# The first stage of the kernels' transform with cosines and sines in one matmul, and a store in four parts

## The chip, the cores and the metric

The kernel runs on one core of a Trainium2 chip. The metric is the device time of one execution in microseconds; lower is better. A profile is one execution taken by the hardware profiler; its span runs from the first to the last recorded work.

## What is computed

A state-space convolution and a gated unit work on the same normalised input and are added to it. L is 2048, D 448, N 256, F 1792.

```python
xn = layernorm(x)                                   # [1, 2048, 448]
P = exp((A * dt[:, None])[:, :, None] * pos)        # A, C complex [448, 256]
K = 2.0 * einsum("dn,dnl->dl", C, P).real           # one kernel of 2048 taps per channel
y = irfft(rfft(xn.T, 4096) * rfft(K, 4096))[:, :2048].T + xn * D_skip
h = sigmoid(xn @ w_gate) * (xn @ w_up)
out = x + y + h @ w_down
```

## The kernel before

Two generators are woven into one program: conv() makes the kernels K and convolves, glu() does the gated unit. A planner takes the next piece from the one whose share of its planned work is smaller, and a scheduler then sets the order of each engine's instructions from priorities and estimated times. An engine runs its instructions strictly in that order. The matmuls of glu() (gu on L685, po on L792) thus fill TensorE between those of conv().

kgen() makes the kernels in 56 chunks of 8 channels. A chunk takes phases from DRAM by matmul (tr, L517), gets sines and cosines of them on ScalarE (S, L526 to L529), magnitudes from GpSimd and ScalarE (me, mf, pm), products on VectorE (Et on L579 and L580, Ft on L581), and sums over N by matmul into a bank ko of PSUM (L593). S is made one chunk ahead of its use.

Four chunks, 32 channels, fill a bank; there are 14 banks. ScalarE copies ko to ks (L606), and first_stage(bank) (L532 to L551) does the first step of the kernels' Fourier transform. The 2048 taps are 32 values of a times 64 of b. ks has 64 r + 32 j + a on partitions, and 8 groups s of 64 values of b, so a channel of the bank is (s, r, j). A matmul holds ks[rows, s], 64 x 64, in the array and streams wk[rows, cc], 64 rows x 64 columns: for the two channels j the 32 frequencies k of a table, which is cosines for cc = 0 and sines for cc = 1. The results go to two banks of PSUM, kp for r = 0 and kq for r = 1, at partitions 64 cc + b. Each matmul of float32 is two instructions in the profile. Two copies on ScalarE (L550) put them into sk as [128, k, (s r j)], 32 x 32, and one store on ScalarE's queue (L551) writes sk to sk_d[:, bank], 4 KB per partition.

spectra() begins after the last bank. Its step for k = 4, ..., or the single step 32, is fed by loads() through SP's queue: sx (x1_d, the transform of the input), tb (a table), and skl (sk_d; 7 banks, four frequencies, 32 channels: runs of 512 B, L849). Step 32 reads one frequency of the rows 64 to 127 in two loads of 64 x 7 x 32 (L841). Step 32 is the second of 17, and its loads are the first that read the last bank. loads() runs three steps ahead. there() multiplies tb with skl and sx (sp, L874), ScalarE and VectorE form the product of the spectra, and back() and last() transform back.

The names that the change touches: sk, sk_d, pss (kp and kq) and first_stage in kgen(); skl, loads() and there() in spectra().

Of the kernel before, what the change touches and what calls it, by code (L numbers as in the profile page):

```python
# [11 lines left out]
F32 = mybir.dt.float32  # L12
# [8 lines left out]
D = 448  # L21
# [28 lines left out]
NLD = 3  # L50
# [80 lines left out]
def s4d_glu_kernel(ctx, tc, io):  # L131
    nc = tc.nc
# [6 lines left out]
    dram = ctx.enter_context(tc.tile_pool(name="dram", bufs=1, space=DRAM))  # L139
    acc_d = dram.tile([128, 8, D], F32, name="acc_d")  # L140
    ph_d = dram.tile([D, 6, N], F32, name="ph_d")
    x1_d = dram.tile([64, NB, D], F32, name="x1_d")
    sk_d = dram.tile([128, D // 32, 32, 32], F32, name="sk_d")
    wt_d = dram.tile([2, NFT, 128, 8 * 128], F32, name="wt_d")

    v_d = dram.tile([2, 128, 32, H], F32, name="v_d")
# [5 lines left out]
    wk = const.tile([128, 2, 128], F32, name="wk")[:, :, :64]  # L152
# [25 lines left out]
    psg = ctx.enter_context(tc.tile_pool(name="psg", bufs=1, space=PSUM))  # L178
# [257 lines left out]
    def kgen(pk):  # L436
        fts, mls, sins = [], [], []

        late = [
            ("sk", [128, 32, 32], F32), ("ks", [128, 8, 64], F32),  # L440
            ("me1", [128, 4 * DC, 64], F32), ("mf1", [128, 4 * DC, 32], F32),
            ("S1", [128, 5, 2 * DC, 32], F32), ("Et1", [128, 2, 2 * DC, 64], F32),
            ("Et0", [128, 2, 2 * DC, 64], F32), ("Ft", [128, 2, 2 * DC, 32], F32),
# [4 lines left out]
        tl = {n: pk.tile(sh, dt_, name=n) for n, sh, dt_ in late}  # L448
# [82 lines left out]

        def first_stage(bank):  # L532

            ks, sk = tl["ks"], tl["sk"].rearrange("p k (s r j) -> p r k s j", r=2, j=2)

            pss = [
                psc[-1].tile([128, 8, 2, 32], F32, name="kp", bufs=1),
                psg.tile([128, 8, 2, 32], F32, name="kq", tag="gu", bufs=4),
            ]
            for s_ in range(8):  # L540
                for cc in range(2):
                    for r in range(2):
                        rows = slice(64 * r, 64 * r + 64)
                        nc.tensor.matmul(  # L544
                            pss[r][64 * cc : 64 * cc + 64, s_].rearrange("p j k -> p (j k)"),
                            ks[rows, s_], wk[rows, cc], start=True, stop=True,
                            skip_group_check=True,
                        )
            for r in range(2):
                nc.scalar.copy(sk[:, r], pss[r].rearrange("p s j k -> p k s j"))  # L550
            nc.scalar.dma_start(sk_d[:, bank], tl["sk"])  # L551

        with hp(HP):
            phase_load(0)
# [8 lines left out]
        for g in range(NCK // NCH):  # L563
            for c in range(NCH):
# [23 lines left out]
                for q in range(2):  # L588
                    sl = 2 * (cn % 4) + q
                    for k in range(4):  # L590
                        h, cc = k // 2, k % 2
                        for j in range(4):
# [4 lines left out]
                                start=(k == 0),  # L597
                                stop=(k == 3),
                                skip_group_check=True,
                            )  # L600
                if cn % 4 == 3:
                    ks = tl["ks"]
# [5 lines left out]
                if cn % 4 == 2 and cn > 3 or cn + 1 == NCK:  # L608

                    with hp(HP) if cn + 1 == NCK else tc.issue_after(glu_mm[0].ins):  # L610
                        first_stage((cn - 3) // 4 if cn + 1 < NCK else cn // 4)
# [202 lines left out]
    def spectra(pf):  # L814
# [15 lines left out]
        def work(n, sh, bufs):  # L830
            return spare[n].pop() if spare[n] else pf.tile(sh, F32, name=n, bufs=bufs)


        def loads(h, k):
            sx = pf.tile([128, 4, H], F32, name="sx", bufs=NLD)
            sk = pf.tile([128, 7, 4, 32], F32, name="skl", bufs=NLD)
            if k == 32:

                nc.sync.dma_start(sx[:64, 0:2].rearrange("b h d -> b (h d)"), x1_d[32])
                for i in range(2):  # L840
                    nc.sync.dma_start(sk[:64, :, i], sk_d[64:, 7 * i : 7 * i + 7, 0])  # L841
                return t32, sk, sx
            ds, gs = slice(H * h, H * h + H), slice(7 * h, 7 * h + 7)
            nc.sync.dma_start(sx[0:64], x1_d[k : k + 4, :, ds].rearrange("k b d -> b k d"))
            nc.sync.dma_start(sx[64:128], x1_d[32 + k : 36 + k, :, ds].rearrange("k b d -> b k d"))
            tb = pf.tile([128, 4, 128], F32, name="tb", bufs=NLD)
            nc.sync.dma_start(tb, io["c_tab"][k // 4])

            nc.sync.dma_start(sk, sk_d[:, gs, k : k + 4])  # L849
            return tb, sk, sx  # L850

        def bank(name):
            return psc[-1].tile([128, 2, H], F32, name=name, tag="sp", bufs=4)

        def after():
            return tc.issue_after(sp_mm[0].ins)

        def there(k, tb, sk, sx):

            kk, np_ = (64, 64) if k == 32 else (128, 128)  # L860
            ys_ = []
            for j in range(2):

                ks = [(0, j, 0)] if k == 32 else [(2 * j + i, 2 * j + i, i) for i in range(2)]
                pss = []
                for src in (sk, sx):
                    ps = bank("sp")
                    with after():
                        for c in range(2):
                            for t, n, i in ks:  # L870
                                to, rhs = ps[64 * i : 64 * i + 64, c], sx[:kk, n]
                                if src is sk:
                                    to, rhs = to.rearrange("p (g d) -> p g d", d=32), sk[:kk, :, n]
                                mm = nc.tensor.matmul(  # L874
                                    to, tb[:kk, t, 64 * c : 64 * c + 64], rhs, start=True, stop=True,
                                    skip_group_check=True,
                                )
                    sp_mm[:] = [mm]
                    pss.append(ps)
                    if src is sk:  # L880
                        kc = work("kc", [128, 2, H], 3)
                        nc.scalar.copy(kc[:np_], ps[:np_])
                yy, pd = work("yy", [128, 2, H], 4), work("pd", [128, 2, H], 2)
                xt = pss[1]
                v.tensor_tensor(yy[:np_], kc[:np_], xt[:np_], ALU.mult)
                v.tensor_tensor(pd[:np_], kc[:np_], xt[:np_, ::-1], ALU.mult)
                v.tensor_tensor(yy[:np_, 0], yy[:np_, 0], yy[:np_, 1], ALU.subtract)
                v.tensor_tensor(yy[:np_, 1], pd[:np_, 0], pd[:np_, 1], ALU.add)
                ys_.append(yy)
            return ys_  # L890
# [63 lines left out]

        steps[0:2] = [steps[1], (None, 32), steps[0]]
        ld = [loads(*s) for s in steps[:NLD]]
        nc.gpsimd.dma_start(wf, io["c_wf"])
        prev, wait, due = None, [], []
        sp_mm[:] = glu_mm
        for n, (h, k) in enumerate(steps):  # L960

            sp_mm[:] = glu_mm
            if prev is not None:
                back(*prev)
            cur = there(k, *ld[n])
            if n + NLD < len(steps):
                ld.append(loads(*steps[n + NLD]))
            if 4 <= n < 8:
                o = slice(2 * n - 8, 2 * n - 6)
                nc.sync.dma_start(ac[:, o], acc_d[:, o])  # L970
            if due and n >= due[0]:
                for m in (0, 2, 4, 6)[2 * (n - due[0]) : 2 * (n - due[0]) + 2]:
                    last(0, m)
                if n == due[0] + 1:
                    due = []
            if prev is not None and prev[1] < 32:
                wait.append(prev[:2])

            while len(wait) > 1 and not (due and wait[0][0] == 1):
                t = wait.pop(0)  # L980
                turned(*t)
                if t == (0, 28):
                    due = [n + 1]
            prev = (h, k, cur)
            glu_on[:] = [1]
            yield WS
# [5 lines left out]
    def conv():  # L992
        with tc.tile_pool(name="psk", bufs=1, space=PSUM) as ps_, tc.tile_pool(
# [78 lines left out]
            with tc.tile_pool(name="pk", bufs=1, side="right", reuse_waits="tile") as pk:  # L1072
                yield from kgen(pk)
# [9 lines left out]
    xq, psc, raws, acl, marks, slots, pqs = list(x_first), [], [], [], [None, None], {}, []  # L1083
# [6 lines left out]
    while any(g is not None for g in gens):  # L1090
# [3 lines left out]
        i = min(live, key=lambda i: done[i] / total[i])  # L1094
# [33 lines left out]
```

## Time and profile before

| what | us |
|---|---|
| median of 3 runs | 756.99 (754.02 to 760.32) |
| the profiled execution | 754.25 |
| its span | 752.5 |

| engine | busy us | share |
|---|---|---|
| TensorE, matmuls | 702.7 | 93% |
| TensorE, loads of weights | 553.0 | 73% |
| VectorE | 560.3 | 74% |
| ScalarE | 423.2 | 56% |
| GpSimd | 346.2 | 46% |

The mean granted clock of TensorE was 0.983 of full speed. In the profile PE is the matmuls of TensorE, PEld its loads of weights, DVE VectorE, ACT ScalarE, POOL GpSimd, SP the SyncE; a q behind an engine's name means its instruction queue, as in ACTq for a DMA that ScalarE issues. Issuing a DMA is not counted as busy. The lines of a group have the form: line, engine, operation, output <- inputs, count, durations. The durations of matmuls are modelled from start to end and overlap, so the distance between starts says more than the duration of one. q10 in the table of DMA queues carries the DMAs that ScalarE issues, q1 those of SP, q0 those of GpSimd.

### The profile page before, as it was taken

The numbers are of one execution on the slowest core, as the hardware profiler recorded it, in microseconds if no ns is written. First come the engines' busy times: TensorE is split into PE (matmuls) and PEld (weight loads), VectorE is DVE, ScalarE is ACT, GpSimd is POOL, SyncE is SP. The second block draws the span as 40 slices with busy tenths as digits, with TensorE's granted clock in tenths as the row PEclk, the third lists the DMA queues.
The fourth block names the chain that finished last, engine by engine and source line by source line (L and its number), as shares of the span: only waits on it lengthen the run. The fifth ranks groups of instructions, "written<-read, shape, count | busy, mean of one in ns | idle before, by whom it ended". The sixth has DMA issues, their size and how long they took to land.

```text
span 752.5 us, 19365 instructions
## 1 busy us (share of the span) xinstructions
PE 702.7 (93%) x7892; PEld 553.0 (73%) x7892; DVE 560.3 (74%) x776; ACT 423.2 (56%) x650; POOL 346.2 (46%) x423
## 2 busy tenths in 40 slices
PE   2897999988998999999999999999899999998994
PEld 2675888766876788655888888888777787776783
DVE  5799996897878898888578968977864555564553
ACT  3546374767677778977487677676643222322310
POOL 2100055995484867863557566566545001341001
PEclk9999999997999999999999999999999999999998
DMA  9945457234223433465852222131158999999746
GB/s 205 232 136 156 121 158 220 68 127 157 70 71 127 156 122 115 123 181 155 245 163 98 74 103 91 64 101 63 49 152 246 255 250 239 240 246 242 184 125 170
DMA packets 90761, 114.75 MB, mean 152 GB/s; under 512 B 11889, under 2 KB 78641, under 8 KB 90417
## 3 DMA queue, kind: packets, MB, share of 16 engines
q1 hardware_dynamic: 81360, 92.78, 45.2%
q10 hardware_dynamic: 6736, 14.57, 6.4%
q0 software_dynamic: 2576, 6.17, 3.1%
q8 instruction: 62, 1.02, 0.6%
q14 instruction: 27, 0.21, 0.1%
HBM read 69.64 MB, written 43.84 MB: 151 GB/s over the span
## 4 chain that ended last, share of the span: by engine, by line
PE 62%; DMA 13%; DVE 10%; ACT 5%; issue 3%; POOL 3%; SPq 2%; POOLq 0%; ACTq 0%; DVEq 0%
PE gu L685 25%; PE po L792 13%; PE tr L517 7%; PE ko L593 6%; PE sp L874 4%; PE pv L901 3%; DMA sx<-x_d 2%; DMA vp<-v_d 2%; DVE hl L703 1%; DMA skl<-sk_d 1%; DMA xe<-in_A_u_dram 1%; DMA tb<-in_c_tab_dram 1%; PE kp L544 1%; DMA v_d<-vt 1%; DMA aim<-in_A_A_imag_dram 1%
## 5 line engine op out<-in xcount | busy, mean ns | idle before, releaser
L494 POOL TENSOR_TENSOR me<-me,pm 128x32 f32<-128x32 f32 (+1 forms) x168 | 138.3, 823 | 111.0 <-DVE Et L580 91.5
L494 POOL TENSOR_TENSOR mf<-mf,pm 128x64 f32<-128x64 f32 (+1 forms) x112 | 107.5, 960 | 4.2
L685 PE MATMUL gu<-xh,wh 128*128 128x512 f32 x336 | 99.8, 404 | 2.2 <-DVE xl L213 2.2
L685 PE MATMUL gu<-xh,wl 128*128 128x512 f32 x336 | 96.6, 393 | 0.0
L685 PE MATMUL gu<-xl,wh 128*128 128x512 f32 x336 | 96.1, 391 | 0.0
L579 DVE TENSOR_TENSOR Et<-me,S 128x1024 f32<-128x1024 f32 x56 | 77.1, 1378 | 17.9 <-ACT S L529 17.9
L580 DVE TENSOR_TENSOR Et<-me,S 128x1024 f32<-128x1024 f32 x56 | 77.1, 1376 | 16.1 <-ACT me L507 12.3
L792 PE MATMUL po<-dh,hh 128*128 128x448 f32 x224 | 85.0, 379 | 2.6 <-DVE hf L696 1.3
L526 ACT ACTIVATE S<-tr 128x1024 f32<-128x1024 f32 x56 | 57.6, 1028 | 52.4 <-PE tr L517 47.0
L581 DVE TENSOR_TENSOR Ft<-mf,S 128x1024 f32<-128x1024 f32 x56 | 81.0, 1446 | 6.4 <-ACT S L529 4.1
L792 PE MATMUL po<-dl,hh 128*128 128x448 f32 x224 | 82.9, 370 | 0.0
L792 PE MATMUL po<-dh,hl 128*128 128x448 f32 x224 | 81.9, 367 | 0.0
L685 PEld LDWEIGHTS gu<-xh,wh 128*128 128x128 f32 x336 | 61.5, 190 | 20.6 <-issue 4.4
L593 PEld LDWEIGHTS ko<-Et,Ft 128*32 128x32 f32 x3584 | 55.1, 112 | 27.5 <-issue 16.9
L701 ACT CAST hh<-hf 128x512 fp32r<-128x512 f32 x56 | 35.0, 625 | 70.3 <-DVE hf L696 59.0
L685 PEld LDWEIGHTS gu<-xh,wl 128*128 128x128 f32 x336 | 63.3, 189 | 14.4 <-issue 0.7
L593 PE MATMUL ko<-Et,Ft 128*32 128x64 f32 x3584 | 65.6, 224 | 8.7 <-DVE Ft L581 4.8
L685 PEld LDWEIGHTS gu<-xl,wh 128*128 128x128 f32 x336 | 62.8, 188 | 14.1 <-issue 0.7
L696 DVE SCALAR_TENSOR_TENSOR hf<-th,gu 128x512 f32<-128x512 f32 x56 | 38.1, 681 | 40.6 <-PE gu L685 37.1
L797 DVE SCALAR_TENSOR_TENSOR acc<-po,acc 128x448 f32<-128x448 f32 x80 | 48.5, 618 | 25.9 <-PE po L792 25.7
L517 PE MATMUL tr<-sel,ph 128*128 128x512 f32 x224 | 66.6, 418 | 1.1 <-ACT S L528 0.6
L529 ACT ACTIVATE S<-S,hpi 128x1024 f32<-128x1024 f32 x56 | 65.5, 1169 | 0.0
(186 smaller groups left out, 1299.4 us busy)
## 6 DMA issues: line engine op xcount, KB each, us to landing
sk_d<-sk ACTq DMA_DIRECT2D x14, 512.0 KB
sx<-x_d SPq DMA_DIRECT2D x32, 224.0 KB
skl<-sk_d SPq DMA_DIRECT2D x16, 448.0 KB
vp<-v_d SPq DMA_DIRECT2D x16, 448.0 KB
v_d<-vt SPq DMA_DIRECT2D x62, 112.0 KB
wt_d<-wh SPq DMA_DIRECT2D x9, 512.0 KB
wt_d<-wl SPq DMA_DIRECT2D x9, 512.0 KB
wh<-wt_d SPq DMA_DIRECT2D x9, 512.0 KB
```

Of the source, the lines that this page charges most:

```text
L494: ins = nc.gpsimd.tensor_tensor(m[:, :, w + a : 2 * w : n], m[:, :, a:w:n], par(base + i).unsqueeze(2).to_broadcast([128, 4 * DC, w // n]) ...
L517: nc.tensor.matmul(ps[:, h], ph[:, cn % 2, 128 * h : 128 * h + 128], sel[:, i], start=(i == 0), stop=(i == 1),)
L526: nc.scalar.activation(rows(cs), pv, AF.Abs)
L529: sins[:] = [nc.scalar.activation(cs, cs, AF.Sin, scale=-TWO_PI, bias=hpi)]
L579: v.tensor_tensor(Et[:, :, :, 32:64], two(me[:, :, 32:64]), S[:, 1::-1], ALU.mult)
L580: v.tensor_tensor(Et[:, :, :, 0:32], two(me[:, :, 0:32]), S[:, 1:3, :, ::-1], ALU.mult)
L581: fts[:] = [v.tensor_tensor(Ft, two(mf), S[:, 3:5], ALU.mult)]
L593: mm = nc.tensor.matmul(ko[32 * j : 32 * j + 32, sl], Ft[:, cc, DC * h + 4 * q + j], Et[:, cc, DC * h + 4 * q + j], start=(k == 0), stop=( ...
L685: glu_mm[:] = [nc.tensor.matmul(ps, a_, b_, start=(n == 0), stop=(n == len(mm) - 1))]
L696: marks[1] = v.scalar_tensor_tensor(hf, th, 1.0, pgu[1], ALU.add, ALU.mult)
L792: glu_mm[:] = [nc.tensor.matmul(po, a_[:, bs], w_, start=(n == 0), stop=(n == 3 * fc - 1))]
L797: v.scalar_tensor_tensor(acc[:, b], po, 0.5, acc[:, b], ALU.mult, ALU.add)
```

## The change

A matmul of the first stage streams the cosines and the sines of a pair of channels together, 128 columns, behind one load of ks. The partitions of PSUM now tell halves of the channels apart (hf, groups s 0 to 3 and 4 to 7) and the free dimension holds cc; before it was the other way round. So there are 16 matmuls of 128 columns a bank in place of 32 of 64. The copies go to sk as [128, cc, k, 16 channels]. Rows of sk_d are still 64 cc + b, so four stores per bank, one for each hf and cc, put the parts where they belong: 64 partitions, 8 runs of 64 elements each. Within a bank sk_d is now 8 groups of four frequencies, two halves, 4 x 16. A step of loads() still reads runs of 512 B; step 32 takes four loads with runs of 16 elements in place of two with 32. there() streams 14 runs of 16 channels per frequency in place of 7 of 32.

```diff
-    sk_d = dram.tile([128, D // 32, 32, 32], F32, name="sk_d")
+    sk_d = dram.tile([128, D // 32, 8, 2, 64], F32, name="sk_d")
...
-            ("sk", [128, 32, 32], F32), ("ks", [128, 8, 64], F32),
+            ("sk", [128, 2, 32, 16], F32), ("ks", [128, 8, 64], F32),
...
-            ks, sk = tl["ks"], tl["sk"].rearrange("p k (s r j) -> p r k s j", r=2, j=2)
+            ks, sk = tl["ks"], tl["sk"]
             pss = [
-                psc[-1].tile([128, 8, 2, 32], F32, name="kp", bufs=1),
-                psg.tile([128, 8, 2, 32], F32, name="kq", tag="gu", bufs=4),
+                psc[-1].tile([128, 4, 2, 64], F32, name="kp", bufs=1),
+                psg.tile([128, 4, 2, 64], F32, name="kq", tag="gu", bufs=4),
             ]
-            for s_ in range(8):
-                for cc in range(2):
+            for s_ in range(4):
+                for hf in range(2):
                     for r in range(2):
                         rows = slice(64 * r, 64 * r + 64)
                         nc.tensor.matmul(
-                            pss[r][64 * cc : 64 * cc + 64, s_].rearrange("p j k -> p (j k)"),
-                            ks[rows, s_], wk[rows, cc], start=True, stop=True,
-                            skip_group_check=True,
+                            pss[r][64 * hf : 64 * hf + 64, s_], ks[rows, 4 * hf + s_], wk[rows],
+                            start=True, stop=True, skip_group_check=True,
                         )
             for r in range(2):
-                nc.scalar.copy(sk[:, r], pss[r].rearrange("p s j k -> p k s j"))
-            nc.scalar.dma_start(sk_d[:, bank], tl["sk"])
+                nc.scalar.copy(
+                    sk.rearrange("p c k (s r j) -> p r c k s j", r=2, j=2)[:, r],
+                    pss[r].rearrange("p s c (j k) -> p c k s j", j=2),
+                )
+            for hf in range(2):
+                for cc in range(2):
+                    s_ = slice(64 * hf, 64 * hf + 64)
+                    nc.scalar.dma_start(
+                        sk_d[64 * cc : 64 * cc + 64, bank, :, hf], sk[s_, cc].rearrange("p (g k) e -> p g (k e)", k=4)
+                    )
...
-            sk = pf.tile([128, 7, 4, 32], F32, name="skl", bufs=NLD)
+            sk = pf.tile([128, 7, 2, 4, 16], F32, name="skl", bufs=NLD)
...
-                    nc.sync.dma_start(sk[:64, :, i], sk_d[64:, 7 * i : 7 * i + 7, 0])
+                    for hf in range(2):
+                        nc.sync.dma_start(sk[:64, :, hf, i], sk_d[64:, 7 * i : 7 * i + 7, 0, hf, :16])
...
-            nc.sync.dma_start(sk, sk_d[:, gs, k : k + 4])
+            nc.sync.dma_start(sk.rearrange("p g h k e -> p g (h k e)"), sk_d[:, gs, k // 4].rearrange("p g h e -> p g (h e)"))
...
-                                    to, rhs = to.rearrange("p (g d) -> p g d", d=32), sk[:kk, :, n]
+                                    to = to.rearrange("p (g d) -> p g d", d=16)
+                                    rhs = sk[:kk].rearrange("p g h k e -> p (g h) k e")[:, :, n]
```

## The prediction

> **What bounds the kernel now.** I read the page's busy times and its 40 slices first, then the table of busy time by stage, then the waits, then single banks of the first stage in the timeline.
>
> ```profile
> span 752.5 us, 19365 instructions
> PE 702.7 (93%) x7892; PEld 553.0 (73%) x7892; DVE 560.3 (74%) x776; ACT 423.2 (56%) x650; POOL 346.2 (46%) x423
> ...
> DMA  9945457234223433465852222131158999999746
> ```
>
> TensorE is busy in 93% of the span: matmuls of the gated unit fill whatever the convolution leaves free. The 49.8 us without a matmul are what a change of order or of a wait can move; else only less work on TensorE helps. The DMA engines are at 9 tenths only at the beginning and from slice 31 on. The stages, as start:end of the stretch, then PE, PEld, DVE, ACT and POOL busy, clock, DMA share, GB/s:
>
> ```profile
> 170.00:220.00 50.00, 46.55 (x718) 38.36 (x722) 38.52 (x36) 34.41 (x48) 28.87 (x35) 0.90 0.30 100
> 220.00:270.00 50.00, 46.39 (x629) 37.54 (x619) 43.51 (x46) 37.70 (x55) 31.54 (x36) 0.97 0.41 139
> 270.00:320.00 50.00, 48.85 (x804) 38.19 (x806) 43.91 (x49) 43.59 (x66) 40.53 (x45) 1.00 0.39 114
> ...
> 420.00:470.00 50.00, 49.96 (x751) 40.76 (x750) 39.34 (x40) 37.13 (x52) 30.68 (x38) 1.00 0.30 98
> ...
> 565.00:626.00 61.00, 61.00 (x416) 46.86 (x417) 31.37 (x63) 17.23 (x33) 10.20 (x13) 1.00 1.01 254
> 626.00:677.00 51.00, 50.95 (x416) 38.57 (x413) 31.36 (x60) 13.69 (x26) 17.88 (x21) 1.00 1.04 239
> ```
>
> The fourteen banks of the first stage lie between 171 and 565. In the first 150 us of that TensorE is idle for 3.45 + 3.61 + 1.15 = 8.2 us, and ScalarE is busy for 115.7 us (77%). From 420 to 470 TensorE is idle for 0.04 us: there a late ScalarE is covered. From 565 on the DMA engines are full and TensorE is full too.
>
> **The matmuls of the first stage.** A bank has 32 matmuls of 64 columns of wk, in the profile 64 instructions; after it has 16 of 128 columns. The groups (count: shortest, median, longest duration in ns):
>
> ```profile
> L544 PE MATMUL kp<-wk,ks x448: 218/218/366, 171.3 to 563.9; 64*64 64x64 f32 x150
> ...
> L874 PE MATMUL sp<-skl,tb x256: 352/353/403, 569.3 to 722.4; 128*64 128x224 f32 x128
> ```
>
> The last bank in the chain of waits (start, us, what):
>
> ```profile
> 563.23 0.04 PE kp L544
> 563.29 0.04 PE kp L544
> ...
> 564.05 0.04 PE kp L544
> 564.11 5.23 PE gu L685 x22
> ```
>
> From 563.23 to 564.05 there are 15 such pieces, 0.82 us from the first to the last, so a set of four (kp and kq, two halves of the columns of the array, side by side) takes 0.82 / 14 = 58.6 ns, and 16 sets 938 ns. From 64 to 224 moved columns an instruction grows by 352 - 218 = 134 ns, 0.84 ns a column: 64 columns are 54 ns of the 58.6. So the set is held by what is streamed, not by its four loads of weights, and the streamed columns stay the same (8 sets of 128). With the same 5 ns of overhead a set takes 112 ns and a bank 898 ns: 40 ns less, **-0.6 us** over 14 banks. The bounds are 0 and, if a set of 128 took no longer than one of 64, 14 x 8 x 58.6 ns = -6.6 us. I take the near end, because the slope between the two groups was seen and the halving was not.
>
> **The copies out of PSUM.** Both kernels make two copies of 128x512 per bank; only the order of the walk differs (innermost runs of two elements, as before).
>
> ```profile
> L550 ACT COPY sk<-kp x14: 619/636/676, 180.6 to 564.2; 128x512 f32<-128x512 f32 x14
> L550 ACT COPY sk<-kq x14: 607/640/677, 181.0 to 564.7; 128x512 f32<-128x512 f32 x14
> ```
>
> I cost this at nothing; ten per cent either way would be 28 x 0.064 = 1.8 us of ScalarE's time, mostly beside other work.
>
> **The store on ScalarE's queue.** One issue of 128 rows of 4 KB becomes four issues of 64 partitions x 8 runs of 256 B. None of that form is in the trace. The nearest rows (ns):
>
> ```profile
> L551 ACTq DMA_DIRECT2D sk_d<-sk x14: 326/327/355, 181.7 to 565.3; - x14
> L670 ACTq DMA_DIRECT2D x_d<-x x32: 452/554/1386, 314.1 to 359.6; - x32
> L844 SPq DMA_DIRECT2D sx<-x_d x16: 613/618/2643, 543.4 to 699.6; - x16
> L849 SPq DMA_DIRECT2D skl<-sk_d x16: 365/412/587, 550.9 to 699.0; - x16
> ```
>
> I take 554 ns, the store of 64 partitions from the same queue; the ends are 365 and 618. Four are 2.2 us (1.5 to 2.5) against 0.33: +1.9 us a bank, +27 us of ScalarE's queue in all. How much of it is hidden is read from a bank of the middle:
>
> ```profile
> 439.24 0.62 ACT L550 COPY sk<-kq 128x512 f32<-128x512 f32 x1
> 439.75 1.03 ACT L526 ACTIVATE S<-tr 128x1024 f32<-128x1024 f32 x1
> 439.89 0.33 ACTq L551 DMA_DIRECT2D sk_d<-sk  x1
> 440.66 1.03 ACT L527 ACTIVATE S<-tr 128x1024 f32<-128x1024 f32 x1
> 441.56 0.61 ACT L528 ACTIVATE S<-tr 128x512 f32<-128x512 f32 x1
> 442.04 1.18 ACT L529 ACTIVATE S<-S,hpi 128x1024 f32<-128x1024 f32 x1
> ```
>
> In the program the issue stands behind L528, yet it ran at 439.89, while L526 was running: the sequencer hands three activations on and issues while they run. Until L529 starts at 442.04 there are 2.15 us of cover, and four issues of 554 ns end at 442.1. In the built changed kernel six of the fourteen banks (the seventh to the twelfth) have just this order, three activations and then four issues: exposed 0.1 us each (0.4 with 618 ns), in a stretch where TensorE has no gaps. I cost those at nothing; without the cover they would be 6 x 1.9 = 11 us of ScalarE's delay.
>
> The first six banks are another matter. There the scheduler has put the four issues in pieces among th, hh, me and the activations of the phase, up to three in a row with a single activation ahead. Queued behind them are me (which the products Et wait for), S (which Et and Ft wait for) and th and hh of the gated unit. Their bounds are 0 and 6 x 1.9 = 11.4 us. ScalarE is 77% busy there and TensorE already has gaps, so some goes through. I take a third, **+3.8 us**, which is a choice. The last two banks hold back th by up to 1.9 us, with the 22 matmuls of gu of the row above running beside it for 5.23 us: **+0.3 us**, bounds 0 and 2.
>
> The order of TensorE also differs between banks two and six (which gu or po stands beside which ko), a shuffle that the 8.2 us of gaps bound on the good side and about as much on the other; I take 0 for it.
>
> **The store in the DMA engines.** Three stretches of the queue table (packets, MB, share of 16 engines): 181 to 186 us, only the store of bank one; 97 to 100.5, loads of 512 B; 570.5 to 572.2, mostly loads of 128 B.
>
> ```profile
> q10 hardware_dynamic: 144, 0.52, 26.2%
> ...
> q1 hardware_dynamic: 1029, 0.49, 50.1%
> ...
> q1 hardware_dynamic: 553, 0.14, 50.5%
> ```
>
> A packet of the store takes 0.262 x 5 x 16 / 144 = 146 ns, one of 512 B 0.501 x 3.5 x 16 / 1029 = 27 ns, one of the third stretch 25 ns. So short packets have a floor near 25 ns. 2048 packets of 256 B are then 2048 x 27 / 16 = 3.5 us of all engines instead of 1.3: +2.2 us a bank at a DMA share of 0.3 to 0.4, and nobody waits for it, except after the last bank. The loads of skl keep 512 B runs. The two small loads of step 32 become four with runs of 64 B: at 25 ns 896 more packets are 1.4 us in all, and SP issues two more (some 0.6 us each).
>
> After the last bank SP stands until the store has landed. SP's issues in the timeline (start, us), the row of its waits (total, times, longest), and TensorE's third step of the spectra in the chain:
>
> ```profile
> 551.93 18.17 SPq L841 DMA_DIRECT2D skl<-sk_d  x2
> ...
> 572.12 0.43 SPq L849 DMA_DIRECT2D skl<-sk_d  x1
> ```
>
> ```profile
> SPq L841 <- DMA sk_d<-sk: 16.9, 1, 16.9
> ```
>
> ```profile
> 587.03 3.18 PE sp L874 x32
> ```
>
> Three more issues of ScalarE (1.7 us), 2.2 us of transfer, partly beside each other, and one more issue of SP after the wait put everything behind it on SP's queue (sx, tb, skl, the accumulators) 3 to 5 us later. The skl issued at 572.12 is used at 587.03, 14.9 us later, so this is hidden: 0, with an upper end of 3 us, since the engines are full from here on.
>
> The Trainium skill, DMA: Bandwidth & Descriptors, section Specifications, puts line rate at 512 B and more and says that below that the engine reads, modifies and writes. By it a 256 B packet of the store would take more than the 27 ns of a load; no row here has a store below 512 B, so the sum keeps 27 ns, and the other reading is a rival below.
>
> **Sum.** -0.6 + 3.8 + 0.3 = +3.5 us. The profiled execution took 754.25 us (span 752.5), 2.7 below the median of 756.99; on the profiled one the sum gives 757.8, on the median **760.5 us**.
>
> **Rivals.** (1) Loads of weights do bind, and a set of 128 costs little more than one of 64: -6.6 us, with issues well hidden 750.4. For it: 73% of PEld; against it: 54 of 58.6 ns are streaming. 12%, a quarter of it beyond 1%. (2) Slower: ScalarE's issues go through. Price: the first six banks whole (11.4) and the last two at most 2, less 0.6, so 766 to 770. It decides when TensorE's gaps between 170 and 320 grow from 8.2 to over 16 us. For it: ACT 43.59 of 50 us busy in 270 to 320; against it: me and S are made a chunk ahead. 20%. (3) Stores of 256 B cost double, 54 ns: 7 us a bank; the last store lands some 8 us later, the third step's skl is issued near 580, and with the engines full it comes late for 587: 4 to 6 us on top of the sum, 765 to 767. The page's rule above speaks for it; no row does. 12%. (4) The new order of banks two to six closes gaps: 8 us less, under 749. 5%. That the change does not take place can be left out: the built program has half the matmuls, each 64x128.
>
> My forecast, 754 to 764.5, has 51%. Within 1% of 756.99 (749.4 to 764.6) is about what a measurement of this kernel can tell from no change: 51% plus 9% of rival 1. Faster by more: 3% of rival 1 and rival 4, 8%. Slower by more: rivals 2 and 3, 32%. The range of 751 to 770 us leaves out most of rival 4, part of rival 1 and the worst of rival 2.
>
> **What would show it.** L544 at about 350 ns a piece but a bank still 0.9 us long: the streaming is right; 0.5 us would be rival 1. Issues of L551's successor at 0.5 to 0.6 us each, 56 of them, and in the middle L529 starting within 0.4 us of L528's end. TensorE's busy time between 170 and 320 near 138 to 142 of 150 us; under 134 is rival 2. The wait of SP's small load of step 32 ending 3 to 5 us after its present place; 8 or more, with waits of sp for skl, is rival 3. I am wrong if the loss lies after 565 with ScalarE on time, or if the copies out of PSUM have grown.

## The result, and the profile after

Timed beside each other, 20 runs each, the kernel before took 758.32 us (median; 753.91 to 765.33) and the changed one 762.56 us (757.19 to 767.71). The ratio is 1.0062, with a 95% interval of 1.0041 to 1.0084. On the 756.99 us of the forecast that is 4.7 us more, where 3.5 us were predicted. Medians here are of all runs, while ratios leave out the few runs that were over 1.5% longer than the fastest of the same kernel (three of twelve at most), so a ratio isn't always the quotient of the medians beside it.

The profiled execution of the changed kernel took 766.09 us, 3.5 above its median; that of the kernel before took 754.25, 4.1 below the 758.32. So the two profiles lie 11.8 us apart, and 7.6 of them are the spread between executions. A stretch in which the profiles differ is therefore a place to look at, and its size is no price.

The granted clock by slices of the kernel before, then the page of the changed one, its busy times, the granted clock and the DMA share by slices:

```profile
PEclk9999999997999999999999999999999999999998
```

```profile
span 764.2 us, 18528 instructions
...
PE 711.0 (93%) x7444; PEld 555.0 (73%) x7444; DVE 561.1 (73%) x776; ACT 423.0 (55%) x650; POOL 338.4 (44%) x423
...
PEclk9999999998999999989899999999999999999998
DMA  9945447135235453544853242331259999999745
```

There are 448 fewer matmul instructions, and TensorE is busy for 8.3 us more. ScalarE and VectorE are busy within 1 us of before, GpSimd 8 us less. The clock is at 8 tenths in slices 18 and 20 (325 to 344 and 363 to 382 us), where it was at 9 before. The stages as start:end of the stretch, PE, PEld, DVE, ACT and POOL busy, clock, DMA share, GB/s; first the stretch from 320 to 370 us of the kernel before, then the changed kernel:

```profile
320.00:370.00 50.00, 48.34 (x598) 32.02 (x587) 36.69 (x50) 34.56 (x59) 28.21 (x40) 1.00 0.65 184
```

```profile
170.00:220.00 50.00, 45.65 (x602) 37.66 (x603) 39.92 (x36) 36.56 (x53) 32.41 (x37) 0.93 0.41 112
220.00:270.00 50.00, 45.55 (x590) 36.43 (x588) 41.63 (x43) 36.19 (x53) 33.52 (x36) 1.00 0.45 137
270.00:320.00 50.00, 46.14 (x658) 34.28 (x658) 42.34 (x48) 36.66 (x56) 27.25 (x35) 0.97 0.43 108
320.00:370.00 50.00, 48.01 (x574) 31.09 (x573) 37.84 (x49) 38.12 (x63) 25.96 (x35) 0.86 0.53 143
...
420.00:470.00 50.00, 49.81 (x666) 41.23 (x665) 39.37 (x45) 34.87 (x50) 31.36 (x43) 1.00 0.32 82
...
565.00:626.00 61.00, 60.14 (x470) 45.58 (x470) 33.41 (x56) 17.78 (x33) 13.81 (x15) 1.00 1.00 236
```

From 170 to 320 TensorE is idle for 4.35 + 4.45 + 3.86 = 12.7 us, against 8.2 before. In the next 50 us the clock is 0.86 against 1.00, and busy time at that clock is not full work. From 420 to 470 TensorE is as busy as before.

Where the two executions part is seen best in one event that every bank has: ScalarE's copy of kp. Start, us, engine, line, first of the kernel before (banks three, six, seven and twelve), then of the changed one:

```profile
247.88 0.65 ACT L550 COPY sk<-kp 128x512 f32<-128x512 f32 x1
...
346.75 0.68 ACT L550 COPY sk<-kp 128x512 f32<-128x512 f32 x1
...
380.16 0.63 ACT L550 COPY sk<-kp 128x512 f32<-128x512 f32 x1 [0.25 <-PE kq L544]
...
525.83 0.62 ACT L550 COPY sk<-kp 128x512 f32<-128x512 f32 x1 [1.78 <-PE kq L544]
```

```profile
242.29 0.65 ACT L551 COPY sk<-kp 128x512 f32<-128x512 f32 x1
...
353.45 0.67 ACT L551 COPY sk<-kp 128x512 f32<-128x512 f32 x1
...
390.46 0.63 ACT L551 COPY sk<-kp 128x512 f32<-128x512 f32 x1 [1.48 <-PE kq L546]
...
536.20 0.63 ACT L551 COPY sk<-kp 128x512 f32<-128x512 f32 x1 [1.59 <-PE kq L546]
```

The changed kernel is 5.6 us ahead at bank three, 6.7 behind at six, 10.3 behind at seven and 10.4 behind at twelve. It neither gains nor loses in the later banks, though each of them has the new matmuls, the copies and the four issues. Between banks three and seven it loses 15.9 us, of which it had gained 5.6 ahead of them. The order of TensorE's instructions is another one from 185 us on. From bank twelve to the end of the span are 228.0 us, against 226.7.

TensorE's time can be divided by stretches of 5 us into idle time, work at full clock (busy time by granted clock) and the rest, which the lower clock took. Of the span of 764.2 us that is 53.2, 696.5 and 14.6; before it was 49.8, 694.9 and 7.8 of 752.5. In the stretch from 280 to 400 us idle and lost time are 12.2 us together, against 2.8, and that is 9.4 of the 11.7 us between these two executions. The sum is given for the experiments too, and how far it can be trusted is seen there.

### The profile page after: what moved, and what is told of

The parts are those of the page before. It is cut to its first block, busy times and chain, and to the rows that moved or that the text cites. A ratio compares the mean times of both kernels' runs of the same rounds, so it can differ in the third digit from the quotient of the medians.

```text
span 764.2 us, 18528 instructions
## 1 busy us (share of the span) xinstructions
PE 711.0 (93%) x7444; PEld 555.0 (73%) x7444; DVE 561.1 (73%) x776; ACT 423.0 (55%) x650; POOL 338.4 (44%) x423
## 4 chain that ended last, share of the span: by engine, by line
PE 56%; DVE 13%; DMA 11%; POOL 6%; ACT 5%; issue 4%; SPq 4%; ACTq 1%; POOLq 0%; DVEq 0%
PE gu L694 23%; PE po L801 12%; PE tr L518 5%; PE ko L602 5%; PE sp L885 5%; POOL me L495 3%; PE pv L912 2%; DVE pm L432 2%; POOL mf L495 2%; DMA v_d<-vt 2%; DVE Ft L590 1%; DVE Et L589 1%; DMA sx<-x_d 1%; DVE Et L588 1%; DMA tb<-in_c_tab_dram 1%
## 5 line engine op out<-in xcount | busy, mean ns | idle before, releaser
L495 POOL TENSOR_TENSOR me<-me,pm 128x32 f32<-128x32 f32 (+1 forms) x168 | 133.6, 795 | 134.8 <-DVE Et L589 116.9
L495 POOL TENSOR_TENSOR mf<-mf,pm 128x64 f32<-128x64 f32 (+1 forms) x112 | 103.9, 928 | 4.5
L589 DVE TENSOR_TENSOR Et<-me,S 128x1024 f32<-128x1024 f32 x56 | 77.8, 1389 | 17.2 <-ACT me L508 13.3
L588 DVE TENSOR_TENSOR Et<-me,S 128x1024 f32<-128x1024 f32 x56 | 74.1, 1323 | 20.2 <-ACT S L530 20.2
L590 DVE TENSOR_TENSOR Ft<-mf,S 128x1024 f32<-128x1024 f32 x56 | 78.6, 1403 | 8.0 <-ACT S L530 5.7
L518 PE MATMUL tr<-sel,ph 128*128 128x512 f32 x224 | 68.2, 427 | 2.2 <-ACT S L529 1.7
```

Source lines behind the costliest of these rows:

```text
L495: ins = nc.gpsimd.tensor_tensor(m[:, :, w + a : 2 * w : n], m[:, :, a:w:n], par(base + i).unsqueeze(2).to_broadcast([128, 4 * DC, w // n]) ...
L518: nc.tensor.matmul(ps[:, h], ph[:, cn % 2, 128 * h : 128 * h + 128], sel[:, i], start=(i == 0), stop=(i == 1),)
L588: v.tensor_tensor(Et[:, :, :, 32:64], two(me[:, :, 32:64]), S[:, 1::-1], ALU.mult)
L589: v.tensor_tensor(Et[:, :, :, 0:32], two(me[:, :, 0:32]), S[:, 1:3, :, ::-1], ALU.mult)
L590: fts[:] = [v.tensor_tensor(Ft, two(mf), S[:, 3:5], ALU.mult)]
```

## The experiments

All were timed in five rounds beside the kernel before, in three groups on three chips; ratios are to the kernel before of the same group (medians of 760.2, 757.55 and 760.04 us).

**One store in place of four.** The first theory was the prediction's own: ScalarE's issues delay its other work. The changed kernel with one issue of 128 partitions x 4 KB a bank; what lands in sk_d is then in halves of channels, and the output differs.

```diff
-            for hf in range(2):
-                for cc in range(2):
...
+            nc.scalar.dma_start(
+                sk_d[:, bank].rearrange("p g h e -> p (g h e)"), sk.rearrange("p c k e -> p (c k e)")
+            )
```

> The changed kernel with its matmuls, copies and loads, but one store of 128 partitions and 4 KB runs per bank (rows of sk_d stay in halves of channels, so the spectra get the parts in another order and the output differs). If ScalarE's four issues cost the time: 0.998 to 1.001 of before, the loss of 0.6% gone. If the matmuls, the copies or the loads of step 32 cost it: 1.005 to 1.007. If the new order of the instructions costs it: anything within 0.7% either way, since this order is a third one.

Measured: 764.83 us, ratio 1.0056 (1.0020 to 1.0091). Without the 42 further issues the loss is still there.

**Four short stores on the kernel before.** The issues, alone: 64 partitions x 8 runs of 256 B, as in the change, on the old layout.

```diff
-            nc.scalar.dma_start(sk_d[:, bank], tl["sk"])
+            for hf in range(2):
+                for u in range(2):
+                    s_ = slice(64 * hf, 64 * hf + 64)
+                    nc.scalar.dma_start(
+                        sk_d[s_, bank].rearrange("p (g u k) e -> p g u (k e)", u=2, k=2)[:, :, u],
+                        tl["sk"][s_].rearrange("p (g u k) e -> p g u (k e)", u=2, k=2)[:, :, u],
+                    )
```

> The kernel before with its one store cut into four of 64 partitions x 8 runs of 256 B to the same places. If the four issues or the short packets cost the time: 1.005 to 1.008 of before, with about 1.9 us more of ScalarE's queue a bank. If the matmuls, copies or loads do: 0.999 to 1.001.

Measured: 758.49 us, ratio 0.9993 (0.9960 to 1.0027). Its issues in the groups (count: shortest, median, longest, ns) and its first three stages, in the columns of the stages above without those of the other engines:

```profile
L554 ACTq DMA_DIRECT2D sk_d<-sk x56: 582/650/1662, 180.4 to 563.9; - x56
```

```profile
170.00:220.00 50.00, 47.44 (x733) 0.94 0.38 96
220.00:270.00 50.00, 46.44 (x611) 0.97 0.44 137
270.00:320.00 50.00, 48.95 (x750) 0.97 0.47 116
```

Fifty-six issues of 0.65 us are 36 us of ScalarE's queue in place of 14 x 0.33 = 4.6, and they cost nothing. TensorE is idle for 7.2 us from 170 to 320, no more than before. The prediction would have read the changed kernel's 12.7 us as the issues; these rows have the same issues and not the gaps.

The four issues bring a new order as well, but in the traces it begins only at 285 us; up to there every engine has the order of the kernel before. From the copy of kp in bank one to that in bank four, all ahead of it, the kernel before takes 98.7 us, this one 98.0. The issues of three banks lie between, three of the six to which the prediction gave its 3.8 us, and with the order held they cost nothing.

**Four long stores.** Four issues again, of 64 partitions x 2 KB, to tell their number from their form.

```diff
...
+                    k_ = slice(16 * u, 16 * u + 16)
+                    nc.scalar.dma_start(sk_d[s_, bank, k_], tl["sk"][s_, k_])
```

> As the one before, four stores of 64 partitions, but one run of 2 KB per partition each; the order of the instructions is that of the kernel with four short stores. If the issues cost: the same 1.005 to 1.008. If the short packets do: 0.999 to 1.001, and the difference of the two is the price of the packets; I expect no difference.

Measured: 756.29 us, ratio 0.9963 (0.9930 to 0.9996), no loss either. TensorE, ScalarE and VectorE have the order of the kernel with four short stores. Neither form of the issues shows a loss.

**Another order of the kernel before.** The rival was that the order makes the difference. WK is the planner's work of a chunk of kernels; another value weaves the same work differently.

```diff
-WK = 5.5
+WK = 5.45
```

> The kernel before, with one number of the planner (the weight of a chunk) 5.45 instead of 5.5: no instruction is added or taken away, only their order differs, as much as between the two kernels. If order alone can move the time: 0.3 to 1% either way. If the issues explain the loss: 0.999 to 1.001.

Measured: 755.52 us, ratio 0.9938 (0.9911 to 0.9966). An order alone is worth as much as the whole effect of the change. Only 5.40 on the kernel before, below, came out with a lower time, in its own group and with a ratio nearer to 1.

**Other orders of the changed kernel, and the pair for each.** If the changed kernel had only drawn an unlucky order, other numbers would scatter about those of the kernel before: WK at 5.45 and 5.40, WP (the work of a piece further back in conv()) at 5.1 for 5, and the kernel before at 5.40.

```diff
-WK = 5.5
+WK = 5.45
...
-WP = 5
+WP = 5.1
```

> The changed kernel with the planner's weight of a chunk 5.45 instead of 5.5, so the same instructions in another order. If the changed code itself costs the time (matmuls of 128 columns, copies, layout, loads): 1.004 to 1.008 of before, as the changed kernel. If the loss is the order, which lowers TensorE's clock between 280 and 400 us: the ratio moves off, to between 0.993 and 1.003, and the clock there is 1.00 in nearly all stretches of 5 us.

> The changed kernel with the weight 5.40, a third order of the same instructions. If the code costs: 1.004 to 1.008. If the order: another value than the two before it, within 0.993 to 1.010, and it follows from the sum of gaps and lowered clock.

> The changed kernel with another number of the planner (the weight of a step of the preparation) 5.1 instead of 5, a fourth order. If the code costs: 1.004 to 1.008. If the order: another value within 0.993 to 1.010.

> The kernel before with the weight 5.40: the spread of orders on the other side. If the code of the change costs, the three changed kernels of this call lie above this one and above the 0.994 of 5.45 by 0.6% each. If the order costs, the two families overlap: this one anywhere from 0.993 to 1.007.

| | before | changed | changed less before |
|---|---|---|---|
| WK 5.5 | 1 | 1.0062 (1.0041 to 1.0084) | 0.6% |
| WK 5.45 | 0.9938 (0.9911 to 0.9966) | 1.0005 (0.9977 to 1.0032) | 0.7% |
| WK 5.40 | 0.9958 (0.9934 to 0.9982) | 1.0043 (1.0013 to 1.0074) | 0.9% |
| WP 5.1 | not run | 1.0022 (0.9989 to 1.0055) | |

Both theories get something. The changed kernel can be had at the time of the kernel before by an order alone, and the ranges of the two overlap. But at the same number the changed one is above in all three pairs, by 0.6 to 0.9%, which speaks against pure chance, though three pairs are few. The two values at 5.45 come from different groups.

What was expected of the clock and the gaps missed. At 5.45 the clock between 280 and 400 us was not 1.00 but 0.97, and TensorE's idle and lost time there was 11.4 us, nearly the 12.2 of the changed kernel, without a loss in the ratio. At 5.40 it was 13.1 and with WP 5.1 14.7, more than in the changed kernel, at lower ratios. So this sum of one execution doesn't give the time of a kernel.

**Everything but the matmuls.** The new layout, copies, four stores and loads, with 32 matmuls of 64 columns.

```diff
-                        nc.tensor.matmul(
-                            pss[r][64 * hf : 64 * hf + 64, s_], ks[rows, 4 * hf + s_], wk[rows],
...
+                for cc in range(2):
...
+                            nc.tensor.matmul(
+                                pss[r][64 * hf : 64 * hf + 64, s_, cc], ks[rows, 4 * hf + s_], wk[rows, cc],
```

> The changed kernel with its layout, copies, four stores and loads, but cosines and sines in two matmuls of 64 columns again, 32 a bank. The scheduler then makes, engine by engine, the order of the run with four short stores. If the copies, the layout or the small loads cost the time: 1.004 to 1.008 of before. If the order that comes with 16 matmuls does: 0.997 to 1.002, as that run.

Measured: 759.27 us, ratio 0.9998 (0.9973 to 1.0023). In the built programs TensorE, ScalarE, VectorE and GpSimd have the very order of the kernel with four short stores, which stood at 0.9993. So at WK 5.5 copies, layout, stores and loads together cost nothing within the interval, and the loss comes with the 16 long matmuls or with the order that they bring. TensorE's gaps from 170 to 320 us were 12.5 us here, as large as in the changed kernel, and 7.2 in the kernel with the same order: they are no price either.

**Long matmuls in one half of the banks.** From that kernel, sets of 128 columns in the last seven banks only, and in the first seven only:

```diff
-                for cc in range(2):
+                for cc in range(2) if bank < 7 else (slice(0, 2),):
```

```diff
-                for cc in range(2):
+                for cc in range(2) if bank >= 7 else (slice(0, 2),):
```

> The changed kernel with 32 matmuls of 64 columns in banks 0 to 6 and 16 of 128 in banks 7 to 13. Up to 400 us the order is that of the run with four short stores; only later the matmuls are long. If long matmuls cost by themselves: 1.002 to 1.004, half of the loss. If the loss is the order between 170 and 400 us: 0.996 to 1.001, with no more than 8 us of gaps and lowered clock from 280 to 400.

> The other way round: 16 matmuls of 128 columns in banks 0 to 6 and 32 of 64 in banks 7 to 13. Up to 400 us the order is that of the changed kernel. If long matmuls cost by themselves: 1.002 to 1.004. If the order: 1.004 to 1.008, the whole loss, with 11 us or more of gaps and lowered clock from 280 to 400.

Measured: late 758.29 us, ratio 1.0001 (0.9960 to 1.0042); early 763.48 us, ratio 1.0060 (1.0030 to 1.0089). The early half carries the loss; the interval of the late one, up to 1.0042, leaves room for a part of it there. In the traces the kernel with late ones has TensorE in the order of four short stores up to 412 us, and the one with early ones has it in the changed kernel's order up to 423. TensorE from 280 to 400 us (busy, clock, DMA share, GB/s), in turn the kernel before, the changed one, late banks, early banks:

```profile
280.00:400.00 120.00, 117.19 (x1530) 1.00 0.54 159
```

```profile
280.00:400.00 120.00, 114.36 (x1394) 0.94 0.56 148
```

```profile
280.00:400.00 120.00, 117.74 (x1584) 0.97 0.59 159
```

```profile
280.00:400.00 120.00, 115.36 (x1398) 0.94 0.56 148
```

The kernels with the same numbers in the planner side by side, from one profiled execution each, in us: the start of the copy of kp in bank seven, from there to the one in bank twelve, from there to the end of the span, and TensorE's idle and lost time from 280 to 400:

| kernel | ratio | bank seven | to twelve | to the end | idle and lost |
|---|---|---|---|---|---|
| before | 1 | 380.2 | 145.7 | 226.7 | 2.8 |
| four short stores | 0.9993 | 379.8 | 145.0 | 228.0 | 5.5 |
| all but the matmuls | 0.9998 | 384.3 | 145.8 | 226.5 | 3.7 |
| long matmuls late | 1.0001 | 383.4 | 145.4 | 227.4 | 5.6 |
| long matmuls early | 1.0060 | 391.0 | 145.8 | 227.0 | 10.9 |
| one store | 1.0056 | 390.9 | 145.9 | 232.1 | 15.2 |
| the change | 1.0062 | 390.5 | 145.7 | 228.0 | 12.2 |

The three kernels that lose are at bank seven 6 us and more behind the four that don't. The five banks from there take 145 to 146 us in all of them, with long matmuls or short ones. The changed kernel at 5.45, with the same long matmuls in another order, is at bank seven at 382.5 and runs at 1.0005.

The copy of bank one comes at 179 to 186 us in these executions, so the way from there to bank seven is the cleaner measure: 198.7 to 200.8 us in the four kernels that don't lose, 206.4 to 208.5 in the three that do. Four long stores, which have the order of four short ones (200.6), took 203.7, so executions of one order differ by some 5 us. The changed kernel took 202.2 at 5.45, 204.3 at 5.40 and 205.9 with WP 5.1, in between, as their ratios are. This way, with what the clock took on it, goes roughly with the ratio; the sum of idle and lost time doesn't.

The loss is not mainly the clock's. The mean granted clock of the twelve runs was 0.974 with short matmuls, with late and with early long ones alike, while the early ones took 4 us longer by the median than the short. The twenty runs of the changed kernel had 0.976, the kernel before 0.976 to 0.978 in the three groups. The spread of the single runs leaves some 2 us either way on that, so at most about half of the 4 us is clock, though the profiled executions of the kernels differ by their clock from 280 to 400.

**The best of both.** Long matmuls late, with WK at 5.45, should have added the free half to the best order of the kernel before.

```diff
-WK = 5.5
+WK = 5.45
...
+                for cc in range(2) if bank < 7 else (slice(0, 2),):
```

> Long matmuls in banks 7 to 13 alone, with the planner's weight 5.45. With that weight the kernel before took 0.994 and the changed one 1.0005. If the order of the early banks is the loss: 0.992 to 0.997, better than both kernels of the change. If the long matmuls, the stores or the loads cost: 0.997 to 1.001.

Measured: 760.7 us, ratio 0.9986 (0.9948 to 1.0023). That missed, and it lies where the expectation had put a cost of the long matmuls, the stores or the loads, 0.5% above the 0.9938 of the kernel before at that number, in another group. So that they are free is shown at 5.5 alone. The order of its early banks is one of its own, not that of the kernel before at 5.45, and it reaches bank seven at 389.3, where that kernel is at 386.5. The gain of an order did not carry over to a program with other instructions.

## Why the prediction was right in its number and wrong in its reason

**The step that failed** is that of ScalarE's issues in the first six banks, "**+3.8 us**, which is a choice". It was by far the largest term of the sum, and the runs show nothing of it: the issues alone run at 0.9993, in the same order the way from bank one to bank four takes 98.0 us with them and 98.7 without, and the change with one issue a bank still takes 1.0056. What took its place comes with the long matmuls of the early banks (1.0060 with them there alone, 0.9998 without any) and lies ahead of bank seven. The only step of the prediction that leaves room for it is the one that got 0: the order of TensorE "between banks two and six", with bounds of 8.2 us each way. The median lies 4.7 us up on the forecast's base, inside those bounds. One term was too high and the other too low by about as much, so that the number was right is luck.

What connects the two is only partly shown. In the built programs 16 matmuls in place of 32 are enough to make the scheduler set TensorE's order anew (from 185 us on in the traces, in the early banks). Four stores alone change it from 294 us on, without loss, and new copies, layout and loads on top of them leave it as it is. Against the long matmul itself being slower speak its rows, below, and the late seven banks, where no loss shows. But no kernel had long matmuls in early banks with the order of the kernel before, so the instruction and its order are told apart by argument there, not by a run. So the cause stays open between the two, and with it why each order that ran with them was 0.6 to 0.9% dearer than its pair.

**The matmuls: right.** The groups of the first stage and three sets of the last bank in the timeline of the changed kernel:

```profile
L546 PE MATMUL kp<-wk,ks x224: 269/269/469, 174.2 to 571.6; 64*64 64x128 f32 x112
L551 ACT COPY sk<-kp x14: 595/630/685, 182.0 to 571.9; 128x512 f32<-128x512 f32 x14
L558 ACTq DMA_DIRECT2D sk_d<-sk x56: 582/648/1606, 183.1 to 575.7; - x56
```

```profile
570.95 0.27 PE L546 MATMUL kp<-wk,ks 64*64 64x128 f32 x1
571.06 0.27 PE L546 MATMUL kp<-wk,ks 64*64 64x128 f32 x1
...
571.61 0.27 PE L546 MATMUL kp<-wk,ks 64*64 64x128 f32 x1
```

From 570.95 to 571.61 there are six sets, 110 ns each, where 112 were predicted and 58.6 would have been rival 1. A bank takes 8 x 110 = 0.88 us in place of 0.94. So streaming holds the set, and loading half the weights gives 0.06 us a bank. The duration of one instruction, guessed at 350 ns, is 269.

**The copies: right.** 630 ns against 636.

**The issues: size and cover.** They take 648 ns, above the 554 taken and the upper end of 618. In the middle the cover held. A bank of ScalarE's timeline (start, us; issues have ACTq):

```profile
450.06 1.04 ACT L527 ACTIVATE S<-tr 128x1024 f32<-128x1024 f32 x1
450.22 1.27 ACTq L558 DMA_DIRECT2D sk_d<-sk  x2
450.98 1.05 ACT L528 ACTIVATE S<-tr 128x1024 f32<-128x1024 f32 x1
451.53 0.65 ACTq L558 DMA_DIRECT2D sk_d<-sk  x1
451.88 0.64 ACT L529 ACTIVATE S<-tr 128x512 f32<-128x512 f32 x1
452.23 0.66 ACTq L558 DMA_DIRECT2D sk_d<-sk  x1
452.93 0.60 ACT L702 ACTIVATE th<-gu 128x512 f32<-128x512 f32 x1 [0.41 <-issue]
```

The four issues run from 450.22 to 452.89 beside three activations, and 0.41 us comes through, as predicted for issues of 618 ns.

**The store's packets: right, rival 3 falls.** From 182.5 to 192 us the queue of ScalarE moved little else than a bank's short packets (packets, MB, share of 16 engines):

```profile
q10 hardware_dynamic: 2112, 0.52, 32.7%
```

That is 0.327 x 9.5 x 16 / 2112 = 23.5 ns a packet, where 27 were taken and 54 would have been the rival. The "floor near 25 ns" for short packets was a misreading, though: by the packet records of the trace before, the 553 packets of its third stretch are 448 of 128 B, which took 13 ns in median, and longer ones, up to 896 B, that raise the mean to 25. The Trainium skill, DMA: Bandwidth & Descriptors, section Specifications, has the engine read, modify and write below 512 B; no time beyond the 27 ns of a 512 B load shows for the packet of 256 B here.

**The wait on SP's queue: right in size, made up otherwise.** The last copy of sk before and the load sx behind step 32, then the last copy of the changed kernel with the issues behind it, and SP's loads of step 32 with what follows (start, us):

```profile
564.66 0.62 ACT L550 COPY sk<-kq 128x512 f32<-128x512 f32 x1
```

```profile
570.14 0.63 SPq L844 DMA_DIRECT2D sx<-x_d  x1
```

```profile
572.45 0.62 ACT L551 COPY sk<-kq 128x512 f32<-128x512 f32 x1
573.11 3.27 ACTq L558 DMA_DIRECT2D sk_d<-sk  x4
576.42 0.60 ACT L702 ACTIVATE th<-gu 128x512 f32<-128x512 f32 x1 [3.35 <-issue]
```

```profile
570.61 0.39 SPq L859 DMA_DIRECT2D skl<-sk_d  x1
578.03 0.47 SPq L848 DMA_DIRECT2D sx<-x_d  x1
578.55 2.63 SPq L851 DMA_DIRECT2D skl<-sk_d  x4
581.22 0.63 SPq L854 DMA_DIRECT2D sx<-x_d  x1
```

The loads of the third step begin at 581.22, 8.1 us after the copy's end at 573.07. Before, the same sx was issued at 570.14, 4.9 us after the copy's end at 565.28. That is 3.3 us later, inside the 3 to 5. The wait for the store itself ends only 0.8 us later behind the copy (5.0 us, at 578.03, against some 4.2, at 570.1 less a load of 0.6); the rest is that sx and all four loads of step 32 now go out behind the wait, where before only the last issue did. No matmul waits for the skl. The th behind the four issues is held for 3.35 us, beyond the "up to 1.9 us" of the prediction. The change with the same stores and loads, but with short matmuls in all banks or in the early ones, shows no loss: 0.9998 and 1.0001.

**The rivals and the signs.** Rival 2 had growing gaps on TensorE, but the wrong cause for them and, with 766 to 770, too high a price. Rival 4 had the place nearly right and the side wrong. Of the prediction's signs one misled: "138 to 142 of 150 us" busy from 170 to 320 came out at 137.3, which looked like a third of ScalarE's issues going through. With the issues alone it was 142.8, and in the same order with everything but the matmuls 137.5, both without a loss. So the sign doesn't tell the causes apart at all.

## What to carry to other kernels

Where a scheduler sets the order, a small edit has two effects: its own, and the new order that it brings; price the second with an interval from orders that are already known (here 0.6% between two orders of the kernel before), and don't explain it by the first. To tell them apart, run each part of the edit alone and the other parts without it, compare the built orders of the pairs, and time a stretch in which the order is still the same. Don't price a kernel by the gaps and the clock of one profiled execution: here they were as large in kernels that lost nothing. Before halving loads of weights, read from two groups of different length whether streaming or loading holds a set.

## What the runs showed of the hardware

A gap of little more than a microsecond on TensorE was followed by half the clock. The changed kernel, TensorE by single microseconds (busy, clock, DMA share, GB/s), and its timeline:

```profile
326.00:327.00 1.00, 0.67 (x3) 1.00 0.25 83
327.00:328.00 1.00, 0.93 (x4) 1.00 0.11 33
328.00:329.00 1.00, 0.04 (x2) 0.99 0.00 0
329.00:330.00 1.00, 0.97 (x4) 0.50 0.00 0
330.00:331.00 1.00, 1.00 (x6) 0.50 0.00 0
...
335.00:336.00 1.00, 1.00 (x8) 0.60 0.85 188
```

```profile
329.03 1.75 PE L273 MATMUL gu<-xt,wx 32*64 32x448 f32 x4 [1.00 <-DVE xl L211]
```

After 1.4 us without a matmul in three, the clock is 0.50 from 329 until after 335: more than 3 us of work lost behind a gap of 1. The Trainium skill, TensorE: Matmul & The Clock Gate, asks in its section "Why this matters for your kernels" for no idle gaps above some 3 us; here the clock fell behind gaps of 1 us and less. That they caused it is not shown, and it isn't a rule: the kernel before was idle for 1.15 us between 325 and 330 and kept its clock, as this row in stretches of 5 us shows.

```profile
325.00:330.00 5.00, 3.85 (x76) 1.00 0.03 8
```

Two things of ScalarE's queue were cheaper than they look: 32 us more of DMA issues cost no time (0.9993), and in the bank shown above they ran beside activations handed on before; and a bank's packets of 256 B took no longer apiece than loads of 512 B (23.5 ns against 27).
